# Tokens turned by plain transposes, logits in the bonus sums' bank, ranks and experts out of one number

## The chip, the core and the metric

The kernel runs on one core of a Trainium2 chip. Its engines are TensorE (PE, with its weight loads as PEld), VectorE (DVE), ScalarE (ACT), GpSimd (POOL) and SyncE (SP, which issues DMAs). The metric is the device time of one execution in microseconds; lower is better.

## What is computed

Three layers in a row, on 4 x 768 = 3072 tokens of width 384 (8 heads of 48):

```python
for t in range(S):                       # linear attention with decay w and a bonus u
    cur = k[t] (x) v[t] * u;  y[t] = r[t] . (state + cur)
    state = w[t] * state + k[t] (x) v[t]
logits = (x / |x|) @ (emb / |emb|).T / tau          # 8 experts
e = argmax(logits);  gate = softmax(logits)[e]
x = gate * (relu(x @ w1[e]) @ w2[e])                 # F = 1024
out = max(x @ m1, x @ m2, x @ m3) @ m_out            # 768 wide
```

## The kernel before

The attention runs over 24 blocks (NG) of 128 tokens, six to a batch row. One pass of the loop `for i in range(-2, NG)` in `attention` works on several blocks at once: it finishes block i, makes the triangular products of block g = i+1, the bonus of block j = i+2 and the turning and scans of block h = i+3. The whole loop stands in a manual schedule: each engine executes its instructions in the order in which the code issues them, and waits only for what they need.

In one iteration TensorE does, in this order: `gram` (L356: products of scaled keys and queries, into the two banks `psA`), the turning of h's decays (L275), `kback` (L372: keys turned back, four transposes), the ranks where there are any, `bonus_sum` (L294: four matmuls over `z`, with `uh`), the turning of h's keys (L275), `outputs` (L410, L417), `bonus_turn` (L302), the turning of h's queries (L275), the list where there is one (L515), `update` (L384) and `tokens` (L426).

- `scan(h)` on VectorE makes `gs` and `es` (L324, L337; 516 columns each, two inputs in SBUF) and `kS`; `scan_r` makes `rt` (L348). `causal(g)` copies the `psA` banks into `AT` under a mask (L362, twice). `carry(i)` adds the state (`S`).
- On GpSimd `diagonal(j)` spreads the bonus `c` over `AT` by a select (L309), and `bonus(h)` multiplies keys and queries into `z` (L288); `carry` has its products `shat` and `Sm` there.
- `tokens(i)` multiplies the outputs `yT` of block i (features in the partitions) by `sel`, a matrix that drops the padding and holds the normed expert embeddings in eight more columns. Out come the block's tokens (`xt`, copied by ScalarE, sent to `xs_d`) and, for each pair of heads, eight partial logits. `logits` (L437) sums these over the four pairs into `dot`.
- Blocks are routed in eight sets (3, 3, 3, 3, 3, 3, 2, 2, and a last 2 by the same functions). `route_expert` makes five VectorE operations (`m`, `e`, `e`, `mx`, `oh`: the one-hot expert), `route_rank` counts ranks on TensorE, `route_slot` makes `cum`, `ro`, `ri`, `rq`, `rl`, `aa`, `ohb`, `pay`, and `route_list` sums the list of tokens by expert on TensorE. The VectorE operations are put into a list, `fillers`; `fill()` issues one of it between causal copies and scans, and `fill(99)`, behind `scan_r` at the end of an iteration, the rest.
- PSUM tiles come from four rings of banks: `A` (2), `T` (2), `Y` (1), `M` (3). `kback`, `bonus_sum`, `update`, `tokens`, `route_rank` and `route_list` take M's three banks in turn; a taker waits until the readers of the tile that held its bank are done. Two engines read a bank one after the other.

Behind the loop VectorE orders the experts by their counts (`order`, `offsets`), SyncE loads the weights of the experts by that order, and from about 205 us on TensorE is occupied with the experts and then the wide layer, which the change doesn't touch.

## Time and profile before

| | us |
|---|---|
| median of 3 runs | 733.84 (733.70 to 734.57) |
| the profiled execution | 733.96 |
| its span on the core | 732.2 |
| TensorE busy | 708.7 (97%) |
| VectorE busy | 428.2 (58%) |
| ScalarE busy | 306.8 (42%) |
| GpSimd busy | 257.0 (35%) |
| attention loop, from the first gram to the last | 13.7 to 179.2 |

Busy shares over the whole span mix the loop, in which all four engines work, with the later layers, in which TensorE works nearly alone. What lies between two instructions of one engine in a stretch, and what it waited for there, is read from the stretch's own rows.

### The profile page before, as it was taken

What the parts mean: (1) busy time and instruction counts of PE and PEld (TensorE: products, weight loads), DVE (VectorE), ACT (ScalarE), POOL (GpSimd) and SP (SyncE); (2) the same over time, 40 slices, a digit from 0 to 9 for tenths busy, and PEclk for the clock granted to TensorE, in tenths of its full rate; (3) what the DMA queues carried; (4) which work ended last, traced back from release to release, by engine and by line L of the source; (5) the groups of instructions that cost most, each with busy time, mean ns of one, the idle gap of its engine ahead of it and who ended that gap; (6) DMA issues with size and microseconds to landing.
All of it is one profiled execution on the core that took longest, in us unless ns stands there. A gap on an engine that the chain in (4) does not pass through costs nothing.

```text
span 732.2 us, 13468 instructions
## 1 busy us (share of the span) xinstructions
PE 708.7 (97%) x4861; PEld 627.6 (86%) x4861; DVE 428.2 (58%) x938; ACT 306.8 (42%) x720; POOL 257.0 (35%) x271
## 2 busy tenths in 40 slices
PE   7999999999799999999999999999999999999994
PEld 4788888888789999999999988988988988889884
DVE  7889999998747986878788368431032031221110
ACT  4667666765445554555556322222121221221120
POOL 6857657476531401201100023343333333223122
PEclk9999999999999999999999999999999999999998
DMA  9997878753365537656554111000100100000001
GB/s 154 171 149 139 138 135 138 144 89 118 104 186 165 170 115 216 202 152 195 152 173 147 60 29 59 23 22 1 44 1 0 44 1 11 33 1 21 22 2 46
DMA packets 146444, 69.05 MB, mean 94 GB/s; under 512 B 104967, under 2 KB 140931, under 8 KB 146360
## 3 DMA queue, kind: packets, MB, share of 16 engines
q1 hardware_dynamic: 141752, 58.27, 35.1%
q0 software_dynamic: 4032, 9.74, 4.2%
q8 instruction: 42, 0.69, 0.4%
q14 instruction: 42, 0.34, 0.1%
q10 hardware_dynamic: 576, 0.01, 0.1%
HBM read 58.52 MB, written 9.48 MB: 93 GB/s over the span
## 4 chain that ended last, share of the span: by engine, by line
PE 85%; DVE 7%; issue 3%; DMA 2%; ACT 1%; POOL 1%; SPq 0%; POOLq 0%; DVEq 0%; ACTq 0%
PE psy L993 16%; PE psT L993 15%; PE psy L933 13%; PE psh L916 13%; PE psh L1017 9%; PE psT L275 4%; PE psA L356 3%; PE psM L426 3%; PE psY L417 3%; PE psY L410 2%; PE psM L384 1%; DMA out_dram<-raw,idx 1%; DVE es L337 1%; PE psM L294 1%; DVE gs L324 1%
## 5 line engine op out<-in xcount | busy, mean ns | idle before, releaser
L999 DVE TENSOR_TENSOR xg<-psT,xg 128x512 f32<-128x512 f32 x18 | 12.4, 690 | 112.8 <-PE psT L993 80.8
L827 DVE TENSOR_TENSOR lw<-raw,hw 128x384 fp32r<-128x384 f32 x120 | 62.3, 553 | 15.8 <-ACT hw L825 14.0
L825 ACT ACTIVATE hw<-raw 128x384 fp32r<-128x384 f32 x123 | 60.7, 524 | 17.7 <-ACT hw L825 10.2
L1007 POOL TENSOR_TENSOR lw<-xg,hw 128x512 fp32r<-128x512 f32 x24 | 31.5, 1311 | 100.4 <-ACT hw L1006 100.4
L841 POOL DMA_INDIRECT xg<-xs_d,idxs x25 | 26.8, 1073 | 111.0 <-PE psT L903 44.6
L1007 POOL TENSOR_TENSOR lh<-xg,hh 128x512 fp32r<-128x512 f32 x12 | 16.1, 1340 | 115.1 <-ACT hh L1006 115.1
L309 POOL TENSOR_SCALAR_AFFINE_SELECT AT<-c 128x1024 f32<-128x1024 f32 x24 | 38.9, 1619 | 49.0 <-ACT c L304 48.9
L1006 ACT ACTIVATE hw<-xg 128x512 fp32r<-128x512 f32 x24 | 15.2, 635 | 97.0 <-DVE xg L1000 97.0
L993 PE MATMUL psy<-yh,mh 128*128 128x512 f32 x162 | 46.7, 396 | 0.2 <-ACT ys L937 0.2
L993 PE MATMUL psy<-yl,mh 128*128 128x512 f32 x162 | 46.6, 395 | 0.0
L993 PE MATMUL psT<-yh,ml 128*128 128x512 f32 x162 | 46.6, 396 | 0.0
L993 PE MATMUL psy<-yh,ml 128*128 128x512 f32 x162 | 46.5, 396 | 0.0
L993 PE MATMUL psT<-yl,mh 128*128 128x512 f32 x162 | 46.5, 396 | 0.0
L993 PE MATMUL psT<-yh,mh 128*128 128x512 f32 x162 | 46.5, 395 | 0.0
L922 DVE SCALAR_TENSOR_TENSOR lh<-psh,hh 128x420 fp32r<-128x420 f32 (+6 forms) x56 | 31.4, 561 | 19.8 <-ACT hh L921 19.5
L916 PE MATMUL psh<-xh,hw 128*128 128x420 f32 (+7 forms) x177 | 42.0, 345 | 0.3 <-DVE lh L922 0.3
L916 PE MATMUL psh<-xh,lw 128*128 128x420 f32 (+7 forms) x183 | 42.0, 339 | 0.0
L1033 POOL DMA_INDIRECT out_dram<-raw,idx x24 | 23.7, 987 | 49.5 <-ACT raw L1023 32.5
L916 PE MATMUL psh<-xl,hw 128*128 128x420 f32 (+7 forms) x177 | 40.7, 337 | 0.0
L933 PE MATMUL psy<-hh,hw 128*128 128x420 f32 (+6 forms) x168 | 40.1, 344 | 0.0
L933 PE MATMUL psy<-lh,hw 128*128 128x420 f32 (+6 forms) x168 | 39.2, 341 | 0.0
L933 PE MATMUL psy<-hh,lw 128*128 128x420 f32 (+6 forms) x168 | 39.2, 341 | 0.0
(329 smaller groups left out, 1801.7 us busy)
## 6 DMA issues: line engine op xcount, KB each, us to landing
raw<-in_moe_w_dram SPq DMA_DIRECT2D x128, 192.0 KB
raw<-in_moe_w_dram SPq DMA_DIRECT2D x18, 384.0 KB
wb<-in_w_dram SPq DMA_DIRECT2D x24, 192.0 KB
kb<-in_k_dram SPq DMA_DIRECT2D x24, 192.0 KB
rb<-in_r_dram SPq DMA_DIRECT2D x24, 192.0 KB
vb<-in_v_dram SPq DMA_DIRECT2D x24, 192.0 KB
xs_d<-xt SPq DMA_DIRECT2D x24, 192.0 KB
raw<-in_moe_w_out_dram SPq DMA_DIRECT2D x6, 384.0 KB
```

The lines of the kernel that those rows point to most:

```text
L275: pe.transpose(t[:112, p * P:(p + 1) * P], flat(src)[:, p * P:p * P + 112], ident)
L309: pool.affine_select(out=x["AT"].rearrange("s q p t -> s (q p) t"), in_=x["c"].rearrange("t q p -> t (q p)").unsqueeze(2).to_broadcast([P, ...
L825: self.act.activation(out=hi, in_=raw, func=AF.Copy)
L827: eng.tensor_tensor(out=lo, in0=raw, in1=hi.bitcast(F32), op=ALU.subtract)
L841: self.pool.indirect_dma_start(out=t[:n], out_offset=None, in_=self.xs_d[0:rows], in_offset=bass.IndirectOffsetOnAxis(ap=self.idxs[:n, 4 * ...
L916: self.pe.matmul(t[:, c0:cap], a[:, d, :], b[:, d, c0:], start=(n == 0), stop=(n == 8))
L922: self.dve.scalar_tensor_tensor(out=lo, in0=t[:, c0:cap], scalar=0.0, in1=hi.bitcast(F32), op0=ALU.max, op1=ALU.subtract)
L933: self.pe.matmul(self.yb[m][:, :cap], a[:, m, :], b, start=(f == 0 and n == 0), stop=(f == 7 and n == 2))
L993: self.pe.matmul(t, a[:, d, f * P:(f + 1) * P], b[:, d, :], start=(n == 0), stop=(n == 8))
L1007: self.pool.tensor_tensor(out=lo, in0=c2, in1=hi.bitcast(F32), op=ALU.subtract)
L1017: self.pe.matmul(t[:, :DM], a[:, c], b[:, f, :], start=(n == 0), stop=(n == 17))
L1033: self.pool.indirect_dma_start(out=self.out, out_offset=bass.IndirectOffsetOnAxis(ap=self.idx2[:, k:k + 1], axis=0), in_=o, in_offset=None ...
```

## The change

Blocks 0 to 20 (`DIRECT` = 21) go the new way, the last three the old one.

- `tokens` turns `yT` by four plain transposes (112 x 128 each) in place of four matmuls with `sel`; ScalarE's copy picks the columns without padding.
- The logits are made by four matmuls more in `bonus_sum`, three blocks later: `enq`, which holds the embeddings in columns 8 to 15 of 32, is multiplied with `yT` into the same bank as the bonus sums. `bonus_turn` turns both at once, and `logits` reads them there.
- `logits` and `route_expert` of these blocks are issued after `bonus_turn` of the same iteration, behind the scans, no longer at the iteration's start.
- `route_rank` makes one chain of n+1 matmuls over all blocks of a set instead of a chain for each block. The counts carry 32 times the expert's number and a doubled rank, so that `rl` and `aa` come out of the one number `ri`; `rq` and the use of `mx` go, and `aa` becomes an operation with one tensor input.
- The counts `cum` lie beside the one-hot tiles in three buffers `ohs`, and one reduction replaces n additions.
- GpSimd's setup makes `twob`, `enq`, a second select on `tri` and an index list more, and leaves out `cum`; ScalarE copies `enq`, VectorE adds to `i32` once.

```diff
+            DIRECT = NG - 3
             def setup3():
                 pool.memset(acc, 0.0)
-                pool.memset(cum, 0.0)
                 pool.memset(oneb, 1.0)
-                pool.affine_select(out=tri, in_=oneb, pattern=[[1, P]], compare_op=ALU.is_gt, fill=0.0,
+                pool.memset(twob, 2.0)
+                pool.memset(enq, 0.0)
+                pool.affine_select(out=tri, in_=twob, pattern=[[1, P]], compare_op=ALU.is_gt, fill=0.0,
                                    base=0, channel_multiplier=-1)
+                pool.affine_select(out=tri, in_=tri, pattern=[[1, P]], compare_op=ALU.not_equal, fill=1.0,
+                                   base=0, channel_multiplier=-1)
...
             def bonus_sum(g):
                 x["cb"] = bank("M", 3)
+                scored = g - 3 if 0 <= g - 3 < DIRECT else None
                 for p in range(NP):
                     pe.matmul(x["cb"][32 * p:32 * p + 32, :P], uh[:, p, :], x["z"][:, p * P:(p + 1) * P],
-                              start=True, stop=True)
+                              start=True, stop=scored is None)
+                if scored is not None:
+                    for p in range(NP):
+                        pe.matmul(x["cb"][32 * p:32 * p + 32, :P], enq[:, p, :], yT[scored % 2][:, p, :],
+                                  start=False, stop=True)
...
             def bonus_turn(g):
-                act.activation(out=x["c"], in_=t.rearrange("t (p q) -> t q p", p=NP)[:, :2], func=AF.Copy)
+                tv = t.rearrange("t (p q) -> t q p", p=NP)
+                act.activation(out=x["c"], in_=tv[:, :2], func=AF.Copy)
+                if 0 <= g - 3 < DIRECT:
+                    st[g - 3]["lv"] = tv[:, 8:16]
...
             def tokens(g):
-                for p in range(NP):
-                    pe.matmul(tv[:, p, :], yT[j][:, p, :], sel[:, p, :], start=True, stop=True)
-                act.activation(out=x["xt"], in_=tv[:, :, :96], func=AF.Copy)
+                if g < DIRECT:
+                    for p in range(NP):
+                        pe.transpose(t[:, p * P:p * P + 112], yT[j][:, p, :], ident[:112, :112])
+                    act.activation(out=x["xt"].rearrange("t p (q d) -> t p q d", q=2),
+                                   in_=t.rearrange("t (p q d) -> t p q d", p=NP, q=2)[:, :, :, :D], func=AF.Copy)
...
             def logits(g):
-                dve.tensor_reduce(out=dot[:, g, :], in_=st[g]["tv"][:, :, 96:104].rearrange("q p e -> q e p"),
-                                  axis=X, op=ALU.add)
+                dve.tensor_reduce(out=dot[:, g, :], in_=st[g]["lv"], axis=X, op=ALU.add)
...
             def route_rank(g0, n):
-                for i in range(n):
-                    o = rk[:, i * E:(i + 1) * E]
-                    pe.matmul(o, oneb, cum, start=True, stop=False)
-                    for k in range(i):
-                        pe.matmul(o, oneb, r["oh"][:, k, :], start=False, stop=False)
-                    pe.matmul(o, tri, r["oh"][:, i, :], start=False, stop=True)
+                pe.matmul(o, twob, r["cum"].unsqueeze(1).to_broadcast([P, n, E]), start=True, stop=False)
+                for k in range(n - 1):
+                    pe.matmul(o[:, k + 1:], twob, r["oh"][:, k:k + 1].to_broadcast([P, n - 1 - k, E]),
+                              start=False, stop=False)
+                pe.matmul(o, tri, r["oh"], start=False, stop=True)
...
             def route_slot(g0, n):
-                def count(i):
-                    return lambda: dve.tensor_tensor(out=cum, in0=cum, in1=r["oh"][:, i, :], op=ALU.add)
+                def count():
+                    with nc.allow_low_precision(reason="small integers"):
+                        dve.tensor_reduce(out=ohs[(r["set"] + 1) % 3][:, 0],
+                                          in_=ohs[r["set"] % 3][:, :n + 1].rearrange("p n e -> p e n"), axis=X, op=ALU.add)
...
-                    lambda: dve.tensor_scalar(out=rq, in0=ri, scalar1=7, scalar2=None, op0=ALU.logical_shift_right),
-                    lambda: dve.tensor_scalar(out=rl, in0=ri, scalar1=4095 - 384, scalar2=None, op0=ALU.bitwise_and),
-                    lambda: dve.scalar_tensor_tensor(out=aa, in0=r["mx"], scalar=-4.0, in1=rq, op0=ALU.mult,
-                                                     op1=ALU.add),
+                    lambda: dve.tensor_scalar(out=rl, in0=ri, scalar1=1, scalar2=4095 - 384, op0=ALU.logical_shift_right,
+                                              op1=ALU.bitwise_and),
+                    lambda: dve.tensor_scalar(out=aa, in0=ri, scalar1=2.0 ** -8, scalar2=HALF, op0=ALU.mult, op1=ALU.add),
...
                 for i in range(-2, NG):
-                    if ok(i - 1):
+                    if i - 1 >= DIRECT:
                         logits(i - 1)
-                    if i - 1 in ends:
-                        fillers.extend(route_expert(*ends[i - 1]))
+                        if i - 1 in ends:
+                            fillers.extend(route_expert(*ends[i - 1]))
...
                     if ok(j):
                         bonus_turn(j)
+                        if 0 <= i - 1 < DIRECT:
+                            logits(i - 1)
+                            if i - 1 in ends:
+                                fillers.extend(route_expert(*ends[i - 1]))
                         diagonal(j)
```

VectorE in the iteration in which a set's experts are chosen (here iteration 6), before: the five operations from `m` to `oh` stand between the causal copies and the scans.

```order
L458 TENSOR_REDUCE m<-dot 128x3
L362 COPY_PREDICATED AT<-msk,psA 128x512
L463 TENSOR_TENSOR e_1127<-dot,m 128x24
L362 COPY_PREDICATED AT<-msk,psA 128x512
L464 TENSOR_TENSOR e_1127<-e_1127,w_156 128x24
L324 SCALAR_TENSOR_TENSOR gs<-wz_145,dG 112x516
L326 RECIPROCAL dE<-gs 112x4
L465 TENSOR_REDUCE mx<-e_1127 128x3
L330 TENSOR_TENSOR kS<-psT,gs 112x512
L466 TENSOR_TENSOR oh<-w_156,mx 128x24
L337 SCALAR_TENSOR_TENSOR es<-wz_145,dE 112x516
L348 TENSOR_TENSOR rt<-psT,es 112x512
```

VectorE in the same iteration, now:

```order
L379 COPY_PREDICATED AT<-msk,psA 128x512 x2
L341 SCALAR_TENSOR_TENSOR gs<-wz_145,dG 112x516
L343 RECIPROCAL dE<-gs 112x4
L347 TENSOR_TENSOR kS<-psT,gs 112x512
L354 SCALAR_TENSOR_TENSOR es<-wz_145,dE 112x516
L460 TENSOR_REDUCE dot<-psM 128x8
L365 TENSOR_TENSOR rt<-psT,es 112x512
L481 TENSOR_REDUCE m<-dot 128x3
L482 TENSOR_TENSOR e_1223<-dot,m 128x24
L483 TENSOR_TENSOR e_1223<-e_1223,w_156 128x24
L484 TENSOR_REDUCE mx<-e_1223 128x3
L485 TENSOR_TENSOR ohs_165<-w_156,mx 128x24
```

The five operations moved together behind `rt`, and `dot`, which stood ahead of the iteration's first copy, stands between `es` and `rt`.

VectorE in the iteration after that, in which ranks are used, from the second scan on, before:

```order
L337 SCALAR_TENSOR_TENSOR es<-wz_144,dE 112x516
L488 TENSOR_REDUCE ri<-ro 128x3
L348 TENSOR_TENSOR rt<-psT,es 112x512
L503 TENSOR_SCALAR rq<-ri 128x3
L504 TENSOR_SCALAR rl<-ri 128x3
L505 SCALAR_TENSOR_TENSOR aa<-mx,rq 128x3
L507 TENSOR_TENSOR ohb<-i_157,rl 128x384
L495 TENSOR_SCALAR pay<-i_158,aa,tid 128x32 x3
```

and now:

```order
L354 SCALAR_TENSOR_TENSOR es<-wz_144,dE 112x516
L528 TENSOR_SCALAR aa<-ri 128x3
L460 TENSOR_REDUCE dot<-psM 128x8
L365 TENSOR_TENSOR rt<-psT,es 112x512
L529 TENSOR_TENSOR ohb<-i_157,rl 128x384
L517 TENSOR_SCALAR pay<-i_158,aa,tid 128x32 x3
```

`aa` moved ahead of `rt`, and `ohb` is the first operation behind it.

TensorE at the end of an iteration with a list and at the start of the next (5 and 6; `sel` and `enq` are the constant matrices, `vb` the values, `kt` the turned keys), before:

```order
L384 MATMUL psM<-vb_123,kt 48x48
L426 MATMUL psM<-sel,yT_151 128x104 x4
L356 MATMUL psA<-rt,kS 128x128 x8
L275 MATMUL psT<-ident,wb_117 112x128 x4
L372 MATMUL psM<-ident,kS 128x112 x4
L294 MATMUL psM<-z,uh 32x128 x4
L275 MATMUL psT<-ident,kb_113 112x128 x4
```

and now:

```order
L401 MATMUL psM<-vb_123,kt 48x48
L444 MATMUL psM<-ident,yT_151 128x112 x4
L373 MATMUL psA<-rt,kS 128x128 x8
L284 MATMUL psT<-ident,wb_117 112x128 x4
L389 MATMUL psM<-ident,kS 128x112 x4
L304 MATMUL psM<-z,uh 32x128 x4
L308 MATMUL psM<-yT_151,enq 32x128 x4
L284 MATMUL psT<-ident,kb_113 112x128 x4
```

The tokens' matmuls became transposes in the same place, and four matmuls joined the bonus sum.

## Rows read from the trace of the kernel before

**Rows 1.** Busy time by stage (window, length, PE PEld DVE ACT POOL, PEclk, DMA share, GB/s)

```profile
5.30:10.10 4.80, 2.68 (x19) 2.16 (x17) 4.33 (x9) 2.78 (x8) 2.73 (x6) 0.99 1.50 167
10.10:13.70 3.60, 3.54 (x23) 2.64 (x23) 2.17 (x5) 1.63 (x5) 0.49 (x1) 0.54 1.51 171
13.70:17.20 3.50, 2.12 (x27) 1.79 (x26) 3.40 (x4) 2.31 (x7) 3.25 (x2) 1.00 1.49 177
...
49.00:92.20 43.20, 42.69 (x532) 36.41 (x531) 40.31 (x89) 28.88 (x77) 28.26 (x46) 1.00 0.80 138
```

**Rows 2.** Chain that ended last, two loop iterations (start, length, what, count)

```profile
36.27 0.39 PE psM L372 x4
...
40.76 1.07 PE psM L426 x8
41.83 1.09 PE psA L356 x16
...
50.83 0.03 PE psM L477
...
50.95 0.36 PE psM L294 x8
```

**Rows 3.** Waits of VectorE, 20 to 192 us (total, times, longest)

```profile
DVE dot L437 <- ACT xt L428: 8.2, 8, 2.5
```

**Rows 4.** Timeline of VectorE, iterations 9 to 12 (start, length, instruction, idle before)

```profile
86.22 0.75 DVE L362 COPY_PREDICATED AT<-msk,psA 128x512 f32<-128x512 int32 x1
...
93.46 0.73 DVE L362 COPY_PREDICATED AT<-msk,psA 128x512 f32<-128x512 int32 x1 [0.18 <-POOL z L288]
...
97.22 1.23 DVE L337 TENSOR_TENSOR_SCAN es<-wz,dE 112x516 f32<-112x516 f32 x1
...
99.39 1.20 DVE L505 SCALAR_TENSOR_TENSOR aa<-mx,rq 128x3 f32<-128x3 f32 x1
...
101.71 1.33 DVE L362 COPY_PREDICATED AT<-msk,psA 128x512 f32<-128x512 int32 x2
...
104.85 1.22 DVE L337 TENSOR_TENSOR_SCAN es<-wz,dE 112x516 f32<-112x516 f32 x1
...
107.47 0.75 DVE L362 COPY_PREDICATED AT<-msk,psA 128x512 f32<-128x512 int32 x1
```

**Rows 5.** Timeline of VectorE, iterations 6 to 8

```profile
64.28 0.75 DVE L362 COPY_PREDICATED AT<-msk,psA 128x512 f32<-128x512 int32 x1
...
70.75 0.75 DVE L362 COPY_PREDICATED AT<-msk,psA 128x512 f32<-128x512 int32 x1
71.79 0.29 DVE L491 TENSOR_TENSOR cum<-cum,oh 128x8 bf16<-128x8 bf16 x1 [0.29 <-PE psM L474]
...
79.57 1.34 DVE L362 COPY_PREDICATED AT<-msk,psA 128x512 f32<-128x512 int32 x2
```

**Rows 6.** Timeline of GpSimd, iterations 2, 9 and 10

```profile
40.26 1.09 POOL L309 TENSOR_SCALAR_AFFINE_SELECT AT<-c 128x1024 f32<-128x1024 f32 x1 [2.84 <-ACT c L304]
...
92.14 1.27 POOL L288 TENSOR_TENSOR z<-kT,rT 112x512 f32<-112x512 f32 x1
...
97.81 1.53 POOL L309 TENSOR_SCALAR_AFFINE_SELECT AT<-c 128x1024 f32<-128x1024 f32 x1 [3.30 <-ACT c L304]
99.31 1.27 POOL L288 TENSOR_TENSOR z<-kT,rT 112x512 f32<-112x512 f32 x1
```

**Rows 7.** Two lines of VectorE, 20 to 192 us (ns min/median/max, first and last)

```profile
L505 DVE SCALAR_TENSOR_TENSOR aa<-mx,rq x9: 161/1201/1206, 56.3 to 191.7; 128x3 f32<-128x3 f32 x6, 128x2 f32<-128x2 f32 x3
L463 DVE TENSOR_TENSOR e<-dot,m x9: 158/167/453, 43.7 to 188.5; 128x24 f32<-128x24 f32 x6, 128x16 f32<-128x16 f32 x3
```

**Rows 8.** Timeline of VectorE at the start

```profile
5.36 0.14 DVE L224 TENSOR_SCALAR enn<-enn 8x1 f32<-8x1 f32 x1 [1.00 <-POOL enn L221]
...
6.81 1.23 DVE L324 TENSOR_TENSOR_SCAN gs<-wz,dG 112x516 f32<-112x516 f32 x1 [0.23 <-ACT wz L277]
```

More of the change, by code (lines that the diff above doesn't have):

```diff
@@ L172, in attention @@
             tri = cp.tile([P, P], BF16, name="tri")
-            cum = cp.tile([P, E], BF16, name="cum")
+            twob = cp.tile([P, P], BF16, name="twob")
+            enq = cp.tile([112, NP, 32], F32, name="enq")
+            ohs = [cp.tile([P, 4, E], BF16, name=f"ohs{i}") for i in range(3)]
             acc = cp.tile([P, 32], F32, name="acc")
@@ L496, in place @@
                                                      scalar2=tid[:, g:g + 1], op0=ALU.is_equal, op1=ALU.mult)
[L499 removed]
+                return ([count] if g0 + n < NG else []) + [
                     lambda: dve.tensor_tensor(out=ro, in0=r["rk"][:, :n * E].rearrange("q (n e) -> q n e", n=n),
```

47 lines of the change are left out of this document (25 added, 22 removed).

## Prediction

> **What bounds the kernel now.** I read the stages first. In the attention loop (one iteration of the order for each of 24 blocks of 128 tokens, from about 20 to 178 us) TensorE is busy 42.69 of 43.20 us, VectorE 40.31 [rows 1]. So TensorE leads, but VectorE has hardly 3 us to spare in six iterations, and the gaps between its instructions take part of that. The waits say the same: from 20 to 192 us VectorE's largest wait is 8.2 us for the logits' reduction (`dot`), in 8 waits [rows 3]. An edit that shortens TensorE's share alone can gain little beyond that. Behind the loop everything is in series (VectorE sorts the counts, the weights of the first experts are fetched by that order, then TensorE is full), so I let a shift at the end of the loop reach the end one for one.
>
> **Three kinds of iteration.** Blocks are routed in sets of three. In the iteration after a set's last block VectorE chooses experts (`m` to `oh`: the expert iteration); in the next TensorE counts ranks and VectorE makes the payload (`cum` to `pay`: the rank iteration); in the third TensorE sums the list (the list iteration). I measure a VectorE cycle from the first causal copy (`AT`, line 362) to that of the next iteration. Before: expert 86.22 to 93.46 = 7.24, rank to 101.71 = 8.25, list to 107.47 = 5.76 [rows 4]; in the set ahead of it 64.28 to 70.75 = 6.47, to 79.57 = 8.82, to 86.22 = 6.65 [rows 5]. Together 43.19 us; the pattern comes twice in full (iterations 6 to 11 and 12 to 17).
>
> **TensorE's part.** Token turning took 1.07 us a block; the transposes that replace it have the shape of line 372's, 0.39. Four more matmuls join the bonus sum, like its own four, 0.36 [rows 2]. Net -0.32 an iteration. Ranks: nine matmuls of some 0.03 us become four, about -0.1 a set [rows 2]. If TensorE stayed the bound: 21 x 0.68 - 21 x 0.36 + 6 x 0.1 = -7.3 us.
>
> **VectorE's part.** Two edits lengthen its cycle.
>
> First, experts. Their five operations stood between causal copies and scans; now all five follow `rt` at the end of the expert iteration, where GpSimd multiplies `z`. The rows show what that means: `AT`'s select on GpSimd took 1.09 us where it ran mostly alone, but 1.53 when it began during VectorE's scan `es`, and ended 0.89 after that scan (97.22 + 1.23 = 98.45; 99.34); `z` followed, and ended at 100.58, 2.13 after the scan [rows 4, 6]. The operation `aa`, 0.16 us at its shortest, was issued at 99.39 and ended at 100.59, with `z`; its median is 1.20. `e`, the second expert operation, goes from 0.16 to 0.45 [rows 4, 7]. Both have two inputs in SBUF. So the new `e` ends where `z` ends, and three dependent operations of 0.16 us with their gaps (0.2 each), then `S` (0.25), stand between that and the next `AT`: 0.85 us behind `z`. In the iteration at 86.22 `z` ended at 93.41 [rows 6]; it can't be much earlier, since the four added matmuls (0.36) delay `c` and so the select, which then runs its 1.09 unheld. Cycle 93.41 + 0.85 - 86.22 = 8.04 for 7.24: +0.8. In the batch-start set (64.28) without operations in between `es` ends after 4.36 (as from 101.71 to 106.07 [rows 4]), plus 2.13 plus 0.85 = 7.35 for 6.47: +0.9.
>
> [...]
>
> Second, ranks. One reduction replaces three additions and a shift goes, about -0.4 ahead of the scan where the additions had to wait (0.29 us at 71.79 [rows 5]), -0.2 where not. But `aa` no longer catches the wait for `z`: `ohb`, two SBUF inputs too, is next and waits instead. End of `z` to next `AT` stays 101.71 - 100.58 = 1.13. Cycles: 8.05 and 8.4 for 8.25 and 8.82. (If the wait spared `ohb`, 0.5 less; I take the wait, by `aa`'s row.)
>
> Third, list iterations. The logits now lie in the bonus sum's bank, which the reduction frees only after `es`. M has three banks, taken in turn; a list iteration takes five (turned keys, bonus sum, list, update, tokens), so its tokens get the bonus sum's bank again and must wait for `dot` of the same iteration. Next stands gram on TensorE, and behind it the next `AT`. So: `AT` to end of `es` 4.36, `dot` and two signals 0.32 (an estimate), transposes 0.39, gram 1.09 [rows 2] = 6.16. Before it was 5.76 where no state update held the bonus sum, so +0.4; and 6.65 where `S` did [rows 4, 5]. There the tensor chain from `S` (signal, eight bonus matmuls 0.75, then keys, outputs, bonus turn, queries, list, update, tokens, gram: some 5.6) gives 6.45: -0.2.
>
> The sum for the six: 7.35 + 8.4 + 6.45 + 8.04 + 8.05 + 6.16 = 44.45 for 43.19: **+1.25**, though TensorE has 1.9 us less to do. Twice: +2.5. First set (iterations 3 to 5): +0.8 - 0.2 + 0.4 = +1.0. Last stretch (18 to 20, where experts and the leader's choice fall in one iteration): +0.9 - 0.4 + 0.75 = +1.25, an estimate from the same cycles.
>
> **The rest.** Iterations 1 and 2, without routing, are TensorE's: 2 x -0.32. At the start GpSimd gets two memsets, a select and an index list more, less one memset, ahead of the power that VectorE's `enn` waits for (1.00 us, until 5.36); that is 0.6 late, and the first scan, at 6.81, had 0.23 us of waiting for something else [rows 8]: +0.4 (0 to 0.6). In the last blocks the old turning stays; four bonus matmuls once, two rank chains shorter: 0. ScalarE's added copy and VectorE's scaling of `i32` lie in waits of over a microsecond at the start: 0. The DMA of the tokens goes out where it did or earlier: 0.
>
> Sum: 2.5 + 1.0 + 1.25 - 0.64 + 0.4 = **+4.5 us**. Against the profiled execution's 733.96 that is 738.5; it stands 0.1 above the median, so **738.4 us**.
>
> **Rivals.**
> 1. *TensorE stays the bound*: VectorE's new waits fall into idle time. -7.3 + 0.4: 727. For it: 97% busy TensorE. Against: VectorE's idle time to be filled is some 8 us in 160 [rows 3], and its cycles above come to 44.45 us where TensorE would need 41.3. Chance 0.07.
> 2. *`z` doesn't hold the moved expert operations* (they slip in ahead of it, or GpSimd gives way). Then expert cycles are -0.3 at 7.24, 0 at 6.47 and 0 in the last stretch; with rank and list cycles as above: first set -0.1, the sixes 2 x -0.65, the last -0.4, and -0.3 for the rest: -2.1, 731.8; with `ohb` spared too, 0.5 x 6 less, 729. It decides from the point where `e`, 0.2 after `m`, is issued before `z`. Against: `z` began at 99.31, 0.07 after `rt`'s end. Chance 0.12.
> 3. *The list wait or the expert wait costs half*: sum 0 to +1.4, no change to be told. Chance 0.15.
> 4. *The tensor clock falls.* New waits stand in front of the tokens, and more of the engine's work is transposes. [...] An iteration at half clock would take TensorE some 13 us for 6.6; ten such, +60: 795. The forecast's longest waits are 1.5 us. Chance 0.03.
>
> [...]
>
> **How the numbers follow.** Forecast 0.63, its own range 735.5 to 741.5 (start term 0 to 0.6, each of 18 cycles to 0.15). The range takes in rival 3 and the upper form of rival 2: 731 to 742; outside are rival 1, part of 2, and 4, below 0.2. A measurement of this kernel can't tell less than 0.2% (1.5 us) from no change. Slower 0.65, same 0.16, faster 0.19.
>
> **What would show it.** In the profile after: `e` at about 1.2 us, ending with `z`, in the expert iterations; `aa` short and `ohb` at 1.5; the token transposes at 0.4 us, with TensorE's wait for `dot` in front of them in every list iteration; grams 22.2 us apart for a set instead of 21.6; TensorE's busy time in the loop some 6 us less. Wrong if `e` stays at 0.16, if no wait for `dot` stands before the tokens, or if six iterations take under 42.5 us.

## The result, and the profile after

The kernel after takes 744.39 us (median of 4 runs, 741.99 to 746.24), the kernel before 734.21 (733.70 to 736.94): ratio 1.0129, 95% interval 1.0088 to 1.0171. Slower was forecast; 738.4 and a range of 731 to 742 were too low, +10.2 us by the medians where +4.5 was said. The profiled execution took 741.99, with a span of 740.3, and stands 2.4 below its median; its span is 8.1 longer than before's. Executions of one kernel differ with the clock that they were granted: over all measurements the kernel before took 733.3 us in the median where its mean granted clock was 0.990 or more (45 executions) and 738.3 where it was below 0.983 (21). The two traces split the 8.1:

| stretch | before | after | difference | forecast |
|---|---|---|---|---|
| start to the first causal copy | 16.78 | 18.02 | +1.24 | +0.4 |
| loop: first causal copy to that of block 22, the last but one | 156.51 | 160.52 | +4.01 | +4.1 |
| from there to TensorE's expert transposes behind the branch (line 929 after, 903 before) | 27.93 | 31.96 | +4.03 | 0 |
| from there to the end | 530.98 | 529.80 | -1.18 | 0 |

So the loop came out as worked out, and about half of the loss lies where I had put nothing. The loop's pieces agree too, so its sum is no luck: iterations 1 and 2 took 0.51 less (0.64 forecast), the first set 0.91 more (1.0), the two patterns of six iterations 1.08 and 1.20 more (1.25 each), the last stretch 1.45 more (1.25). The 4.03 behind it are 1.55 between the last two causal copies (7.56 for 6.01), 0.70 less from there to the sorted counts, and 3.18 from these to the transposes.

The stages of after (the columns of [rows 1]):

```profile
4.80:9.30 4.50, 2.81 (x21) 2.12 (x19) 3.14 (x7) 2.59 (x7) 2.98 (x11) 1.00 1.50 161
9.30:16.10 6.80, 4.69 (x29) 3.63 (x31) 5.46 (x8) 2.90 (x10) 1.35 (x2) 0.50 1.47 178
18.02:178.54 160.52, 146.98 (x1952) 121.92 (x1952) 149.94 (x296) 104.71 (x280) 100.71 (x115) 1.00 0.74 128
49.00:92.20 43.20, 39.79 (x526) 33.16 (x525) 41.00 (x83) 27.84 (x75) 27.44 (x44) 1.00 0.75 137
180.00:185.00 5.00, 5.00 (x48) 4.00 (x48) 1.52 (x6) 0.72 (x3) 2.79 (x3) 0.67 0.86 247
205.00:210.00 5.00, 0.00 (x0) 0.14 (x1) 0.43 (x2) 0.00 (x0) 0.00 (x0) 0.72 0.55 157
```

The whole loop in before:

```profile
16.78:173.29 156.51, 152.58 (x1901) 129.65 (x1902) 145.07 (x315) 104.22 (x280) 101.96 (x116) 1.00 0.77 133
```

Over the loop TensorE is busy 146.98 us where it was 152.58, 5.6 less (some 6 were forecast), and without work for 13.5 where it was 3.9; VectorE is busy 149.94 for 145.07. So the change did take work from TensorE, and TensorE now waits. (The window of 43.20 us holds six iterations of before but not quite six of after, which take 44.28; its 39.79 for 42.69 [rows 1] is no saving in six iterations.) At 205 to 210 TensorE does nothing at all.

VectorE in the loop, iterations 6 to 8 (columns as in [rows 5]):

```profile
65.81 1.37 DVE L379 COPY_PREDICATED AT<-msk,psA 128x512 f32<-128x512 int32 x2 [0.78 <-PE psA L373]
...
71.30 1.26 DVE L482 TENSOR_TENSOR e<-dot,m 128x24 f32<-128x24 f32 x1
...
73.38 0.74 DVE L379 COPY_PREDICATED AT<-msk,psA 128x512 f32<-128x512 int32 x1
...
78.30 0.99 DVE L528 TENSOR_SCALAR aa<-ri 128x3 f32<-128x3 int32 x1
...
79.90 1.03 DVE L529 TENSOR_TENSOR ohb<-i,rl 128x384 fp32r<-128x384 f32 x1
80.86 0.70 DVE L517 TENSOR_SCALAR pay<-i,aa,tid 128x32 fp32r<-128x32 f32 x3
81.48 0.34 DVE L413 TENSOR_TENSOR S<-Sm,psM 112x192 f32<-112x192 f32 x1
81.74 1.34 DVE L379 COPY_PREDICATED AT<-msk,psA 128x512 f32<-128x512 int32 x2
...
88.06 1.38 DVE L379 COPY_PREDICATED AT<-msk,psA 128x512 f32<-128x512 int32 x2 [0.78 <-PE psA L373]
```

and GpSimd beside it:

```profile
71.24 1.27 POOL L297 TENSOR_TENSOR z<-kT,rT 112x512 f32<-112x512 f32 x1
...
77.51 1.76 POOL L326 TENSOR_SCALAR_AFFINE_SELECT AT<-c 128x1024 f32<-128x1024 f32 x1 [2.30 <-ACT c L319]
79.24 1.27 POOL L297 TENSOR_TENSOR z<-kT,rT 112x512 f32<-112x512 f32 x1
```

`e` was issued 0.06 after `z` began and ended with it (72.56 and 72.51): 1.26 for 0.16, as forecast. `aa` ended with the select (79.29 and 79.27), though it has one input; `ohb` (0.56 where nothing holds it, in e6 below) was held by what was left of `z`, until 80.51. The cycles are 73.38 - 65.81 = 7.57, then 8.36, 6.32, 7.89, 7.83 and 6.31, where the forecast had 7.35, 8.40, 6.45, 8.04, 8.05 and 6.16: 44.28 for 44.45.

What TensorE waited for, 20 to 192 us (total, times, longest):

```profile
PE psM L444 <- DVE dot L460: 5.5, 6, 1.1
PE psM L304 <- POOL z L297: 3.4, 5, 1.4
PE psM L496 <- DVE ohs L485: 2.6, 6, 0.5
```

and one of the list waits in its timeline:

```profile
86.26 0.60 PE L444 MATMUL psM<-ident,yT 112*128 112x112 f32 x4 [1.05 <-DVE dot L460]
86.80 1.16 PE L373 MATMUL psA<-rt,kS 48*128 48x128 f32 x16
```

The tokens' transposes stand in front of `dot` once in each list iteration, 1.05 us here, and the gram behind them is what the next `AT` waits for (0.78 at 88.06). The four transposes take 0.60 us, where 0.39 was told.

The new loss lies behind the loop. TensorE's timeline there, after and then before; its weight loads (PEld) in after's stand; and after's DMA packets on the instruction queue q8 in two stretches of 2 us, 204 to 206 and 208 to 210 (packets, MB, share):

```profile
204.26 0.28 PE L902 MATMUL psT<-ml,mh 128*128 128x256 f32 x1
210.50 1.28 PE L929 MATMUL psT<-ident,hw 128*128 128x128 f32 x6 [5.96 <-DVE gsort L1065]
```

```profile
198.16 0.28 PE L876 MATMUL psT<-ml,mh 128*128 128x256 f32 x1
201.22 1.36 PE L903 MATMUL psT<-ident,hw 128*128 128x128 f32 x6 [2.78 <-issue]
```

```profile
206.89 0.14 PEld L929 LDWEIGHTS psT<-ident,hw 128*128 128x128 f32 x1 [2.55 <-issue]
210.50 0.40 PEld L929 LDWEIGHTS psT<-ident,hw 128*128 128x128 f32 x2 [3.47 <-issue]
```

```profile
q8 instruction: 1, 0.02, 3.0%
...
q8 instruction: 1, 0.02, 2.9%
```

TensorE stands 5.96 us where it stood 2.78. VectorE's `gsort`, which the row names, doesn't feed these transposes (in e2 below they start 2.85 us ahead of it). After's stand is two stands: at 206.89 the first weight load of these transposes runs, and then TensorE issues nothing for another 3.47 us. The queue q8 brings one packet after 204 and another after 208. In before the packets come at 198.2 and 201.9, the second behind the stand's end at 201.22; so the packets alone don't tell the two cases apart, and the weight load does. Experiment e2_shift takes this up.

### The profile page after: what moved, and what is told of

Read it like the earlier page. It is cut to its first block, busy times and chain, and to the rows that moved or that the text cites. A ratio compares the mean times of both kernels' runs of the same rounds, so it can differ in the third digit from the quotient of the medians.

```text
span 740.3 us, 13547 instructions
## 1 busy us (share of the span) xinstructions
PE 703.9 (95%) x4909; PEld 620.6 (84%) x4909; DVE 434.0 (59%) x917; ACT 306.8 (41%) x721; POOL 255.7 (35%) x273
## 4 chain that ended last, share of the span: by engine, by line
PE 76%; DVE 14%; issue 3%; DMA 2%; POOL 1%; ACT 1%; SPq 0%; POOLq 0%; ACTq 0%; DVEq 0%
PE psy L1019 15%; PE psT L1019 14%; PE psy L959 13%; PE psh L942 13%; PE psh L1043 8%; DVE es L354 3%; PE psT L284 2%; DVE AT L379 2%; DVE gs L341 2%; PE psA L373 2%; PE psY L434 1%; PE psY L427 1%; DVE kS L347 1%; DVE e L482 1%; PE psT L929 1%
```

## The experiments

Ratios are against the kernel before, measured beside each run; loop times are from the profiled execution (156.51 before, 160.52 after), cut as in the table above. The expectations call the same stretch "first to last causal copy".

| | median us | ratio, 95% interval | loop us |
|---|---|---|---|
| e1_again | 742.40 | 1.0095 (1.0060 to 1.0129) | 160.48 |
| e2_shift | 739.91 | 1.0062 (1.0036 to 1.0088) | 160.48 |
| e3_setup | 743.63 | 1.0104 (1.0070 to 1.0137) | 160.50 |
| e4_list | 739.63 | 1.0053 (1.0030 to 1.0075) | 159.20 |
| e5_expert | 738.50 | 1.0049 (1.0025 to 1.0073) | 156.16 |
| e6_spread | 744.61 | 1.0149 (1.0124 to 1.0173) | 163.69 |
| e7_list2 | 738.87 | 1.0072 (1.0049 to 1.0096) | 157.73 |
| e8_before_moved | 739.27 | 1.0071 (1.0047 to 1.0094) | 157.14 |
| e9_all_moved | 737.33 | 1.0014 (0.9990 to 1.0037) | 157.71 |
| e10_before_spread | 748.76 | 1.0177 (1.0139 to 1.0215) | 168.64 |
| e11_route_alone | 740.57 | 1.0059 (1.0037 to 1.0082) | 159.40 |
| e12_gaps | 743.13 | 1.0094 (1.0067 to 1.0120) | 163.32 |
| e13_no_stand | 734.92 | 0.9993 (0.9963 to 1.0023) | 154.68 |
| e14_tokens_alone | 745.63 | 1.0139 (1.0096 to 1.0181) | 161.06 |
| e15_no_stand_tail | 733.68 | 0.9980 (0.9955 to 1.0006) | 155.13 |

### The stand behind the loop: where the code lies

e1_again is the kernel after, unedited. e2_shift puts 24 matmuls more (48 instructions with their weight loads) into an arm of the branch on the experts' capacities that isn't taken, so that the code behind it lies elsewhere and nothing else is executed:

```diff
-                for _ in range(IDLE[1]):
+                for _ in range(IDLE[1] + (24 if self.caps is CAPS[1] else 0)):
```

e8_before_moved adds 48 matmuls there to the kernel before.

> The changed kernel once more, unaltered, as the base for its neighbours. Theory: its extra time has four places, by the first profile against the kernel before: first causal copy 1.2 us later, attention loop 4.0 us longer, from its last causal copy to the sorted counts 0.9, from the sorted counts to the first transposes of the experts 3.2 (8.85 instead of 5.67 us), and some 1.1 given back later. So about 742 to 746 us, and these four differences again, each within 0.3 us. Rival: the extra time behind the loop is an accident of one execution (a late fetch or a late DMA); then the 3.2 us are not there this time and the time is nearer to 740.

> The changed kernel with 24 more matmuls on the constant tile warm in an arm of the branch on the experts' capacities that this input does not take. Nothing that runs is changed; the code of the arm that is taken moves by some 48 instructions. Theory: TensorE's 5.96 us of idle time in front of the experts' first transposes are two code fetches of 3 us behind the branch, because the arm starts at the very end of a 16 KB fetch; moved, one fetch does: idle time 2.8 to 3.1 us, and the kernel 3 us faster than the unaltered one (about 741.5). Rival: TensorE waits there for data (the gathered tokens or the weights); then idle time and total time stay as they are (744.4).

> The kernel before with 48 more matmuls on the constant tile warm in an arm of the branch that is not taken: nothing that runs is changed, the code of the taken arm moves to where it lies in the changed kernel (to within 2 instructions). Theory of the code fetch: TensorE's idle time in front of the experts' first transposes grows from 2.78 to 5.9 us, and the kernel is 2.5 to 3.2 us slower than before. Rival (a wait for data): no difference.

In e1 three of the four places came again: the start (17.90), the loop (160.48) and 3.00 more from the sorted counts to the transposes. The fourth didn't: from the loop's end to the sorted counts e1 took 21.76 us, less than before's 22.11, where the first profile had 22.96. The difference is the cycle between the last two causal copies, 6.23 in e1 and 7.56 in after, whose granted clock was 0.67 from 180 to 185 (above); e1's was at full speed there (mean clock of the profiled executions: after 0.983, e1 0.986). The ratio of e1 is 1.0095, within the first result's interval.

TensorE's timeline at the first expert transposes, e2 and then e8:

```profile
206.54 0.83 PE L929 MATMUL psT<-ident,hw 128*128 128x128 f32 x6 [2.74 <-issue]
```

```profile
201.41 0.30 PE L903 MATMUL psT<-ident,hw 128*128 128x128 f32 x1 [2.45 <-issue]
205.02 1.17 PE L903 MATMUL psT<-ident,hw 128*128 128x128 f32 x5 [3.31 <-issue]
206.53 1.49 PE L1044 MATMUL psy<-warm 128*128 128x512 bf16 x3 [0.34 <-issue]
```

In e2 the 5.96 are 2.74 again, with the loop unchanged. In e8 the kernel before gets a second stand: one transpose, then 3.31 us without anything to wait for that the trace shows, and the first expert matmul starts 6.05 after the first transpose where it took 2.62. It costs before 0.71% (0.47 to 0.94), 5.2 us by the medians, of which the stand explains 3.4; behind it the half clock lasted 6.8 us where it had lasted 3.4 (before: 0.52 from 201.0 to 204.5). So the position of code that isn't executed decides about some 3.2 us here. That each stand is a fetch of code is read from the q8 packets, from the weight load between the two stands and from "issue"; the trace doesn't name the code that a packet holds. After's page has 43 packets and 0.70 MB on q8, some 16 KB each; that the arm begins at the very end of such a packet, as e2's expectation has it, is not shown. All experiments below but e3 have one stand (e4, e11 and e14 by chance, e10 as before has it, the others with e2's edit).

### The start: who begins second waits

e3_setup moves `oneb`, `twob`, `tri` and the index lists behind the first `bonus`, and `enq`'s memset behind `sel`'s:

```diff
             def setup3():
...
+                pool.memset(enq, 0.0)
+
+            def setup3b():
                 pool.memset(oneb, 1.0)
                 pool.memset(twob, 2.0)
-                pool.memset(enq, 0.0)
```

> The changed kernel with GpSimd's setup of oneb, twob, tri and the index lists put behind the first z, and enq's memset behind sel's; the power that VectorE waits for comes earlier than in either kernel. Theory: the first scan starts at about 6.6 instead of 7.1 us, and the scan es behind it starts before GpSimd's z, so that es takes 1.23 instead of 2.18 us and z is the one that waits; first causal copy at 16.5 to 16.9 us instead of 18.0, total time 1.2 to 1.5 us less (about 743). Rival: the stretches of half tensor clock at the start (10 to 17 us) last as long as before and take the gain back: first causal copy at 17.5 or later, total within 0.4 us of the unaltered kernel.

The second scan and GpSimd's product at the start, before, then after:

```profile
8.29 1.23 DVE L337 TENSOR_TENSOR_SCAN es<-wz,dE 112x516 f32<-112x516 f32 x1
...
8.34 2.25 POOL L288 TENSOR_TENSOR z<-kT,rT 112x512 f32<-112x512 f32 x1 [1.99 <-ACT rT L282]
```

```profile
8.59 2.18 DVE L354 TENSOR_TENSOR_SCAN es<-wz,dE 112x516 f32<-112x516 f32 x1
...
8.42 1.26 POOL L297 TENSOR_TENSOR z<-kT,rT 112x512 f32<-112x512 f32 x1 [1.45 <-ACT rT L291]
```

Here whichever begins second is held until the first is done: before it was `z`, second by 0.05 us (2.25 us for 1.26), after it is `es`, second by 0.17 (2.18 for 1.23). The first scan was 0.31 late (7.12 for 6.81), as forecast; that turned the order round, for 0.95 more. In e3 the scan stands at 6.81, `es` takes 1.23 and the first copy is at 16.77: the 1.24 is back. The time isn't: 743.63 beside 742.40. In e2 `es` took 1.23 too, with the setup unedited, so the order changes from run to run. The single profile shows the 1.24; the medians can't.

### The loop: one wait after the other

e4_list sums the list in bank Y; e7_list2 puts the list behind the next iteration's gram; e5_expert moves the expert operations one iteration on, back between copies and scans, and ranks and list with them; e6_spread puts `rl`, `aa` and `ohb` ahead of `es`. The last three have e2's edit too, so e2 is what they are compared with. The main lines of the four edits, in this order:

```diff
-                pm = r["pm"] = bank("M", 3)
+                pm = r["pm"] = bank("Y", 1)
```

```diff
+                    if i - 4 in ends and i - 4 <= 17:
+                        route_list(*ends[i - 4])
+                        fillers.insert(0, lambda e=i - 4: route_add(*ends[e]))
```

```diff
+                    if i - 2 in ends and i - 2 <= 17:
+                        fillers.extend(route_expert(*ends[i - 2]))
...
-                            if i - 1 in ends:
+                            if i - 1 in ends and i - 1 > 17:
```

```diff
-                    lambda: dve.tensor_scalar(out=aa, in0=ri, scalar1=2.0 ** -8, scalar2=HALF, op0=ALU.mult, op1=ALU.add),
...
+                    spread,
```

> The changed kernel with the list's sum in the bank of the outputs (Y) instead of the ring M; so the tokens of a list iteration no longer get the bank that holds the logits. Theory: the six waits of TensorE for dot in front of the tokens (5.5 us together) go, the causal copy behind them starts when S is done and not 0.78 us later, and the list cycles become 5.6 us instead of 6.31: 3 to 4.7 us faster than the unaltered changed kernel (about 740.5). Rival: the list now waits for ScalarE's copy of yT in bank Y and the time of the list cycles is set elsewhere (rT, z): under 1.5 us.

> The changed kernel with the code moved as in e2_shift (its base) and with the list's matmuls of the sets up to block 17 one iteration later, behind the gram; the tokens then never get the logits' bank, and the list waits for nothing of the same iteration (in e4_list it waited for ScalarE's copy of the outputs). Theory: list cycles fall from 6.31 to 5.6 us, where VectorE alone sets them; the loop 3.5 to 4.2 us shorter, total about 736. Rival: what is gained there is lost in the next cycle, where the expert operations end with z whatever happens ahead of them, and z follows the keys and queries of TensorE: the loop 1.5 us shorter at most.

> The changed kernel with the code moved as in e2_shift (so that run is its base: first to last causal copy 160.48 us) and with the choice of experts of the sets up to block 17 issued at the start of the iteration after, one operation at a time between causal copies and scans as in the kernel before; ranks, list and sum of these sets are each one iteration later too. Theory: e no longer waits for GpSimd's z (0.16 to 0.45 us instead of 0.98 and 1.26), and the expert cycles (7.57, 7.89) lose 0.8 to 1.1 us, of which the short operations put 0.3 to 0.5 back in the next one: the loop 4 to 6 us shorter, total 735 to 737. Rival: the z-bound end of the iteration only moves to the next two-input operation (S or ohb), or TensorE has become the bound: the loop under 2 us shorter.

> The changed kernel with the code moved as in e2_shift (its base) and with rl, aa and ohb issued together ahead of the scan es in the rank iterations, where GpSimd has little to do, instead of around and behind it. Theory: aa (0.99 us, held by GpSimd's select) and ohb (1.03, held by z) fall to 0.16 and 0.42, es starts 0.6 later, and only the three short payload operations stand behind rt: the rank cycles (8.36, 7.83) lose 0.8 to 1.2 us, the loop 5 to 7. Rival: the payload waits for z in their place, or TensorE sets the rank cycle: the loop under 2 us shorter.

The list wait: with the list in another bank its cycles fall from 6.31 to 6.05 only, since another wait takes its place, that of the list for ScalarE's copy of `yT` (e4's waits of TensorE):

```profile
PE psY L537 <- ACT yT L436: 2.7, 6, 0.6
```

With the list behind the gram (e7) they fall to 5.35, but the expert cycles behind them rise from 7.58 and 7.89 to 8.00 and 8.31; the loop gets 2.75 shorter. The expert wait: in e5 the operations take 0.16 to 0.49 again and the loop is 4.3 us shorter, 156.16, as long as before's, though the cycle of iteration 20 has grown to 10.13. So the two waits of the forecast are the loop's loss, and the expert wait is the larger. The total times don't show it: 1.0049 (e5) and 1.0072 (e7) are not clear of e2's 1.0062. In e5's profile 3.3 us of the 4.3 come back behind the expert transposes, where the granted clock was 0.50 from 203.7 to 213.9 and in e2 was not (mean clock of the profiled executions 0.980 and 0.989).

e6 went the other way. VectorE and GpSimd in e6 at the same place:

```profile
77.73 0.56 DVE L519 TENSOR_TENSOR ohb<-i,rl 128x384 fp32r<-128x384 f32 x1
78.20 2.12 DVE L354 TENSOR_TENSOR_SCAN es<-wz,dE 112x516 f32<-112x516 f32 x1
80.24 1.18 DVE L524 TENSOR_SCALAR pay<-i,aa,tid 128x32 fp32r<-128x32 f32 x1
```

```profile
77.95 1.29 POOL L326 TENSOR_SCALAR_AFFINE_SELECT AT<-c 128x1024 f32<-128x1024 f32 x1 [2.29 <-ACT c L319]
79.21 2.18 POOL L297 TENSOR_TENSOR z<-kT,rT 112x512 f32<-112x512 f32 x1
```

`ohb` is no longer held, but `es` now begins 0.25 behind the select and is held in its place, and `z` and `pay` hold each other next. The rank cycles grow by 0.5. Moving the held instruction moved the wait.

### The two halves

e11_route_alone has the routing of after with the old tokens and logits; e14_tokens_alone has the plain transposes and the logits in the bonus bank, with before's ranks and counts.

```diff
-            DIRECT = NG - 3
+            DIRECT = 0
```

> The changed kernel with DIRECT = 0: all tokens turned by the old matmuls, logits with them and experts chosen at the iteration's start as in the kernel before; what is left of the change is the ranks and experts out of one number, the single count and GpSimd's setup (enq is made and not used). Theory: the loss in the loop belongs to the turned tokens with their logits and moved experts, not to this part: loop 154.5 to 156 us, below the kernel before's 156.5 by the 0.2 to 0.4 us of each rank cycle; with up to 1.2 us lost at the start the total is 1 us less to 0.5 more than before. Rival: aa, now early and held by GpSimd's select, costs the rank cycles 0.8 us each: loop 159 or more.

> The kernel before with the first half of the change alone: plain transposes for the tokens of blocks 0 to 20, the logits in the bonus sums' bank, logits and experts issued behind the scans; ranks, counts, aa and setup as before (enq's memset stands behind the power). First to last causal copy: 156.5 us in before, 160.5 with the whole change, 159.4 with the other half alone. Theory that the halves share their waits (both end with z and the list): 159.5 to 161.5. If they add, this half costs the missing 1.1 us: 157 to 158.5. If the turned tokens gain by themselves: under 156. The total follows the loop, with no loss at the start and the code of the branch in a good place.

Routing alone costs the loop 2.9 us, tokens alone 4.55, both together 4.0: they share waits. The routing half was to gain 0.2 to 0.4 a set. Its rows at the ranks of iteration 10 (VectorE, GpSimd, TensorE of e11):

```profile
100.85 1.00 DVE L528 TENSOR_SCALAR aa<-ri 128x3 f32<-128x3 int32 x1
...
102.36 0.54 DVE L529 TENSOR_TENSOR ohb<-i,rl 128x384 fp32r<-128x384 f32 x1
102.82 1.66 DVE L517 TENSOR_SCALAR pay<-i,aa,tid 128x32 fp32r<-128x32 f32 x3
```

```profile
100.42 1.41 POOL L326 TENSOR_SCALAR_AFFINE_SELECT AT<-c 128x1024 f32<-128x1024 f32 x1 [3.19 <-ACT c L319]
101.80 2.23 POOL L297 TENSOR_TENSOR z<-kT,rT 112x512 f32<-112x512 f32 x1
```

```profile
104.08 0.43 PE L304 MATMUL psM<-z,uh 112*32 112x128 f32 x8 [0.61 <-POOL z L297]
```

Before, `aa` waited out the whole of `z` [rows 4, 6], which ran its 1.27 unheld. Now `aa` waits for the select instead, so `ohb` and `pay` come while `z` runs: `z` takes 2.23, the bonus sum waits 0.61 for it, and the list cycle behind grows by 0.5 to 0.6, three times. Here it isn't the second that is held: `ohb` began 0.56 after `z` and took its 0.54, in all six rank cycles of e11, and `z` took 2.23; why is not shown. The other piece is one cycle of 8.31 for 7.24: `w7`, now made by VectorE out of GpSimd's `pos`, waits 2.02 for it once. In after it lies behind the held experts and costs only its own 0.16.

The time of the tokens alone, 1.39% over before, doesn't follow from its loop, as was expected. In its profile (the slowest of its six executions) 6.9 us more than in before lie between the loop's end and the sorted counts (29.0 for 22.1). There VectorE's ranks of a late set fall together with GpSimd's products of the weights: `rl` took 1.04, `aa` 1.03 and `ohb` 1.29 at 190.8 to 194.0, where before had 0.16, 0.16 and 0.85.

### Can the gain on TensorE be had?

e9_all_moved joins e3, e5 and e7 for the sets to block 14 and issues nothing of the routing behind `es`. e10_before_spread spreads the routing in e9's way on the kernel before, with two operations in the first gap. e12_gaps spreads single operations into the gaps of VectorE; e13_no_stand differs from it in `ohb`'s place and in the list, now behind the gram of the iteration after; e15_no_stand_tail is e13 with the new way for blocks 0 to 16. The main lines of e13:

```diff
+                    if early_set(5) and i - 5 < SH:
+                        route_list(*ends[i - 5])
+                    if early_set(3):
+                        route_rank(*ends[i - 3])
+                        c, ro, ri, rl, aa, ohb, p0, p1, p2 = route_slot(*ends[i - 3])
+                        fillers.extend([ro, ri, both(rl, aa, ohb), nothing])
+                        later = [c, p0, p1, p2]
```

> The changed kernel with GpSimd's setup as in e3_setup, the code moved as in e2_shift, and the routing of the sets up to block 14 spread over three iterations: one operation in each gap between S, causal copies, scan gs and kS, none behind the scan es (where GpSimd's select and z run), the list's matmuls behind the gram two iterations after the ranks. Theory: the change's saving on TensorE is real and was covered by VectorE's waits; without them the iterations of the loop go at TensorE's 6.4 to 6.8 us, the loop (first to last causal copy) takes 147 to 151 us for 160.48 in e2_shift and 156.5 in the kernel before, and the time is 6 to 9 us below the kernel before. Rival: another chain (keys and queries to z to the bonus sum, or S to the outputs) holds the iterations at 7 us whatever VectorE does: loop 154 or more, time within 0.4% of before.

> The kernel before with the same spreading of the routing (sets up to block 14, nothing behind es, two operations in the first gap, since it has three more operations a set), old tokens, old logits. It tells the spreading from the change. Theory: here TensorE sets most iterations (42.69 of 43.20 us busy), so the loop gets at most 1 to 2 us shorter (154.5 to 155.5 for 156.5), time 0 to 2 us less than before. Rival: the spreading alone brings what e9_all_moved brings; then the loop is 150 us or less and the transposes had no part in it.

> As e9_all_moved, but by what its rows and those of e6_spread show: of two operations that hold each other on VectorE and GpSimd the later one waits, so a routing operation stands only where GpSimd neither runs nor is about to start: reductions behind S, two-input ones behind the causal copies, the payload's comparisons behind the copies and the reciprocal, nothing behind kS in the rank and payload iterations. Ranks right behind the gram, the list behind the tokens (its ring place then lies behind the logits' reduction without a wait in front of the tokens), and the weights w7 one iteration later, where GpSimd's pos is long there. Theory: no routing operation takes over 0.5 us up to iteration 17 (aa 0.91 and pay 1.09 in e9), a set's three cycles come to 19.8 to 20.6 us for 22.2 in e2_shift and 21.1 to 21.6 before, the loop takes 149 to 153 us for the kernel before's 156.5, and the time is 0.4 to 0.9% below the kernel before. Rival: the cycles are bound by TensorE with z in front of the bonus sum at 7 us; loop 154 or more and no difference from before that can be told.

> As e12_gaps with two steps moved: ohb ahead of kS in the rank iteration, so that in the payload iteration the scan es starts ahead of GpSimd's select (in e12 it started 0.05 us behind it and took 2.13 us); and the list behind the next gram instead of in front of it, so that TensorE never stands for the logits there (1.8 us in e12, after which the tensor clock was 0.5 for 6.8 us). Theory: the stand was the cause of the half clock; without it the clock stays at 1.00 up to iteration 17, six cycles take 41 to 42 us (43.2 before, 44.3 in e2_shift), the loop 147 to 152 us, and the time is 0.5 to 1% below the kernel before. Rival: less work on TensorE between short waits is enough for the clock to fall; then it falls here too, and the loop stays at 155 us or more.

> The kernel of e13_no_stand, with the new way for blocks 0 to 16 instead of 0 to 20: the last blocks' experts, lists and logits are issued where the kernel before has them, and the selects of the set 12 to 14 come ahead of them. Theory (e13's loss lies in its last three iterations, 8.25 + 9.6 + 8.21 = 26.1 us where the kernel before has 22.7, because the late set's work was pushed together there; the gain of the six-cycle patterns is real): the patterns stay near 41.5 us, the last three iterations come back to 22.7 to 24, the loop takes 152 to 153.5 us for 154.68, and the time is 1 to 3 us under the kernel before (0.9960 to 0.9985). Rival (the late set's work has to be done somewhere, and every place in the last iterations is full): the loop stays within 0.7 us of 154.7, and the time within 0.2% of the kernel before. Second rival: with the last blocks' turning back on TensorE's longer form, the last iterations lose more: loop over 155.5.

e9's loop came down to 157.71, not to the 147 to 151 expected. e10 shows that its moves alone aren't what helps: on the kernel before they cost 12 us of loop, part of it by the clock (0.50 for 13.7 us of the loop, in three stretches). e12 ran into the clock. TensorE's timeline in e12, two stretches of its stage view, and then e13's stage view:

```profile
69.25 0.82 PE L545 MATMUL psM<-pay,ohb 128*128 128x32 f32 x3 [1.79 <-DVE dot L465]
70.00 2.08 PE L378 MATMUL psA<-rt,kS 48*128 48x128 f32 x16
```

```profile
62.00:69.20 7.20, 5.46 (x79) 4.17 (x75) 6.61 (x11) 5.86 (x17) 4.80 (x6) 1.00 0.89 155
69.20:76.00 6.80, 6.75 (x49) 5.79 (x50) 4.12 (x11) 1.45 (x4) 2.49 (x4) 0.50 0.83 127
```

```profile
62.00:103.00 41.00, 40.56 (x546) 33.46 (x544) 38.92 (x83) 29.15 (x78) 24.63 (x26) 1.00 0.81 145
...
145.00:171.40 26.40, 23.34 (x295) 19.40 (x291) 24.12 (x57) 15.76 (x43) 15.39 (x16) 0.94 0.29 61
```

Behind a stand of 1.79 us, in a stretch with 5.46 of 7.20 busy, the granted clock was 0.50 from 69.20 to 76.00 and a gram took 2.08 for 1.16; the loop is 163.32 long. Two more such stands, one every six iterations, were followed by half clock from 117.00 and from 161.38 (0.96 over 92.20 to 135.30, 0.95 over 135.30 to 170.00). Without them, in e13, TensorE is busy 40.56 of 41.00 us, the clock stays at 1.00, and six cycles take 41.23 us (62.90 to 104.13) and again 41.26 (to 145.39) for 43.19 before. So the change does shorten the loop, by 1.9 us a pattern of six, where VectorE's waits are out of the way. The order of e13 without the new tokens was not run, but it couldn't reach this: before's TensorE is busy 42.69 us in six iterations [rows 1], more than the 41.23 that e13's take. The last iterations (18 to 20) give it back: 8.25, 9.60 and 8.21 for 6.37, 8.90 and 7.44, and e13 as a whole equals before. e15 had these iterations in before's order and they took 8.71, 9.27 and 7.80; the theory that the order alone was the loss fell. TensorE stands 1.49 us in front of the late list in e13 and 1.38 in front of the keys' turning (`kback`) in e15, and the granted clock falls behind it: 0.94 from 145.00 to 171.40 in both. Of all kernels e15 is the fastest against before, by 0.2% with an interval that holds zero. No version clearly beats the kernel before.

## Why the prediction was wrong in size, point by point

- **VectorE as the bound.** Right. TensorE lost 5.6 us of work in the loop, and the loop grew by 4.0; rival 1 (727) is out. VectorE's room was 11.4 us in the loop (145.07 of 156.51 busy), not some 8. e13 shows the premise from the other side: with the waits gone TensorE is busy 99% and the cycles are near the 41.3 that rival 1 took.
- **Expert iterations**, 7.35 and 8.04: measured 7.57 and 7.89, by the mechanism named (`e` ends with `z`). Rival 2 is out (its cycles for six iterations add up to -0.72, not -0.65, which moves its 731.8 by 0.1); e5 prices the wait at 4.3 us of loop.
- **Rank iterations**, 8.40 and 8.05: 8.36 and 7.83. The end was right: the next copy stood 1.23 behind the end of `z` (1.13 told). What lies ahead of it was not as told. "`aa` short" was wrong: with one input it was held 0.99 by the select, and `ohb`, which so began later, took 1.03 and not 1.5; the two errors offset each other. Alone, the routing half loses (e11).
- **List iterations**, 6.45 and 6.16: 6.32 and 6.31. The wait for `dot` stands where it was put, 5.5 us in 6. The 0.32 for `dot` and two signals was an estimate that no row showed; in after the transposes start 0.22 behind the start of `dot` (86.04 to 86.26). Rival 3 (half the cost) is out.
- **The start**, +0.4 (0 to 0.6): +1.24 in the profile. `enn` was late by 0.63 and the scan by 0.31, as worked out; the step that failed is that this moved `es` behind `z`, 0.95 more. The rows had the margin, but I read `es` and `z` at the start only for what they took, not for the 0.05 us between their starts.
- **"I let a shift at the end of the loop reach the end one for one", the rest 0.** This is the step that made the number miss. +4.03 lie between the loop's end and the experts, 3.2 of them a second stand of TensorE that depends on where the compiled code lies (e2, e8); I took 2.78 us of "issue" before as given and had no term for code that moves. Most of the rest is the last cycle at half clock, which e1 didn't have. 1.18 came back later, so a shift isn't passed on one for one either.
- **Rival 4, the clock.** From the first to the last but one causal copy of after it stayed at 1.00 (18.02 to 178.54), with six groups of transposes an iteration, so the rival is out there. But the clock can fall inside the loop: to 0.50 for 13.7 us in e10, and in e12 from 69.20 to 76.00 behind a stand of 1.79. That transposes have a part in it is not shown. Of after's half-clock stretches, one lies at the start (0.50 from 9.3 to 16.1; before 0.54 from 10.1 to 13.7 [rows 1]), one between the last two causal copies (0.67 from 180 to 185), where it goes with 1.3 us (7.56 for e1's 6.23), and one begins in the stand (0.72 from 205 to 210) and lasts to 214.1.
- **What stays open.** The medians differ by 10.2, the profiles by 8.0, and in e1 the unaltered kernel was 0.95% (0.60 to 1.29) slower. After's four runs lie 4 us apart, before's over all measurements from 731.5 to 740.9, and from the first expert matmul to the wide layer the same code took 214.85 us (after) to 220.88 (e12, whose granted clock was 0.50 from 209.2 to 219.4). The 3.2 us are shown (e2, e8), and of the loop's 4.0 the waits that make them (e5, e7), in the loop but not in the total times. How much of the 2 us between the profiled run and its median is the clock isn't shown: after's four executions don't lie in the order of their clocks (741.99 at 0.983, 743.30 at 0.985, 745.49 at 0.985, 746.24 at 0.980).

## What to carry to other kernels

Where two engines hold each other's instructions, list the start times of both at every place that the edit touches, to a tenth of a microsecond: in nearly all rows here the one that begins second waits for the whole of the first (`z` 2.25 us for 1.26, `es` 2.18 for 1.23; e11's `ohb` is the exception), and an edit that moves one by 0.3 us can turn the order round. Work taken from a full engine was worth nothing here until the other engine's waits were moved out of its way too, and then the stretch where the pattern doesn't hold (the last sets) must be read by itself. After any change in the number of instructions, look at the stands in front of branches behind it; the price there was one of code position here (some 3.2 us, e2 and e8), and a few instructions in an arm that isn't taken told it from the change itself.

## What the runs showed of the hardware that I had not expected

- An operation of VectorE with one tensor input was held by GpSimd: `aa` 0.99 to 1.00 us in after and e11, 0.16 in e6 where GpSimd was idle; `pay` 1.66 in e11 for 0.70 in after. I had reckoned with it only for operations with two inputs, as `aa` and `e` are in before. Why those with one are held is not shown.
- GpSimd is held as well as VectorE: `z` took 2.17 to 2.25 us instead of 1.27 where it began 0.05 to 0.80 us behind `es` (three times in before, twice in after), and 2.23 in e11, where it began first.
- A stand of TensorE behind a branch took 2.5 to 3.5 us, once (before 2.78, e2 2.74) or twice (after 2.55 and 3.47, e8 2.45 and 3.31), by the position of the code.
- Inside the loop single stands of TensorE went with the clock: behind each of three of 1.8 us the granted clock fell to 0.50 (e12, from 69.20 to 76.00 the first time), and without them (e13) it stayed at 1.00 up to a stand of 1.49, while after's, with 3.4 of 43.2 us without work in stands of up to 1.05, stayed at 1.00 (49.00 to 92.20 in the stages above). Stands are not all of it: one of 1.41 us, at 22.7 in after, left the clock at 1.00, and in e10 it fell to 0.50 at 95.2 behind waits of 0.37 and 0.18 us (0.90 over 90 to 125).
